# The loads of batch 0 on three queues, token weights held, and a new order of work in a fused attention and wave-MLP kernel

## The chip, the cores and the metric

The kernel runs on one core of a Trainium2 chip. The metric is the device time of one execution in microseconds (us), as a median of several runs. One execution was also taken by the hardware profiler; all views below are of that one. The engines are PE (matrix multiply, with its weight loads as PEld), DVE (elementwise and reductions), ACT (activation functions and copies), POOL (a slower general engine) and SP (which issues transfers). Transfers are moved by 16 DMA engines. SP issues on a queue that the profile calls hardware_dynamic; POOL issues on software_dynamic, and it spends its own time on each issue.

## The reference

Linear attention over 8 batches, 8 heads, 576 positions, 64 values a head, then a norm for each head, then a wave-like MLP over C = 512 channels:

```python
kv  = einsum('bhsd,bhse->bhde', k, v)
out = einsum('bhsd,bhde->bhse', q, kv)
x   = out / sqrt(mean(out*out, -1) + 1e-6) * g_norm      # then (b, s, h*d)
theta = x @ w_theta
y = einsum('ts,bsd->btd', w_tok_r, x*cos(theta)) + einsum('ts,bsd->btd', w_tok_i, x*sin(theta))
u = x + y
result = u + maximum(u @ w_ch, 0)
```

## The kernel before

Each batch has 576 positions, which are cut into four full tiles of 128 rows and one half-size tile (the 64 left-over positions, folded so that 256 columns stand on 128 rows); `j` counts these five. A tile (b, j) goes through these steps, each a small function that issues the instructions of one engine:

- **Attention.** `kv_piece` (L174) multiplies k by v on PE, two heads at a time, four pieces a batch; `kv_out` copies the sum to `kbd` on ACT. `q_turn` (L198) transposes q on PE, `q_out` (L216) copies it to `qT`, `raw` (L222) multiplies `qT` by `kbd`.
- **Norm.** `square` (L243, ACT), `sums` (L249, DVE), `root` (L257, POOL: the lines L260, L264, L266 make `ss`, `rt`, `gr`), `x_make` (L274, DVE: `x = raw * gr`).
- **Phase.** `x_turn` (PE), `x_out` (copy to `xT`), `theta` (PE, with the weights `wth`), `whole_turns` (`pt`), `reduce_arg` and `even_arg` (DVE, L321 and L329), `sine` and `cosine` (ACT), `z_make` (DVE). The half tile's z goes to a buffer `zf` and is moved into place as `zt` by four small transfers on SP (`z_move`, L361).
- **Token and channel mix.** `token_mix` (PE, `y`) sums nine matrix products over all z of the batch; it reads the transposed token weights `wT` (made by `w_turn` and `w_out`) and needs `zt` in its last third. Then `u_make` (DVE), `u_turn`, `u_out`, `channel_mix` (PE, `v`, weights `wch`), `finish` (DVE) and `store` (SP).

The order of the instructions on each engine is fixed before the kernel is built. Every step is a `Task` with an engine, a planned cost, the tasks that it depends on and a key. `in_order` (L35) plays the tasks forward in planned time: of the tasks that can start first on an engine, the one with the smallest key goes next. Keys are counted in tiles: tile (b, j) has `s = 5 b + j`, and its token mix has `s + LAG`. A transfer is a task on its issuing engine plus one on an imagined `wire` that takes `MB` us per megabyte. On the chip each engine runs its list strictly in order and waits for semaphores; a transfer also waits until one of its kind's eight completion semaphores is free, so the ninth transfer on a kind of queue waits for the first to land, and so does everything behind it on its engine.

The transfers at the start, before: SP issues k and v of batch 0 in turn, then `g_norm` (`g8`), then `w_theta` (`wth_s`), then k and v of batch 1. POOL issues q of batch 0, the token weights in six transfers, q of batch 1, `w_ch`, q of batch 2 and 3. `prep_theta` scales `wth_s` into `wth` on ACT. PSUM rings bound how far PE runs ahead: two `raw` tiles, two tiles of transposes, four of the wide sums.

Of the kernel before, what the change touches and what calls it, by code (L numbers as in the profile page):

```python
# [71 lines left out]
def kernel(  # L72
# [78 lines left out]
    IM = S + TL  # L151

    def load_token(w_in, lo, n, at):
        nc.gpsimd.dma_start(
            out=wn[:, :, at:at + n],
            in_=w_in[0:SM, lo:lo + n].rearrange("(p j) s -> p j s", j=NJ),
        )
        nc.gpsimd.dma_start(out=wnt[:, at:at + n], in_=w_in[SM:S, lo:lo + n])
# [279 lines left out]

    def w_turn(n):
        if n < NJ:  # L440
            cols = slice(IM + n, 2 * S, NJ)
        elif n < 2 * NJ:
            cols = slice(n - NJ, SM, NJ)
        else:
            cols = slice(SM, IM)
        t = ps.tile([P, S], FP16, tag="tr", bufs=2, name="wps")
        for jj in range(NJ):
            nc.tensor.transpose(t[:, jj * P:(jj + 1) * P], wn[:, jj, cols], ident[:])
        nc.tensor.transpose(t[:, SM:S], wnt[:, cols], ident[0:TL, 0:TL])
# [35 lines left out]
    for hp in range(NHP):
        hs = slice(2 * hp, 2 * hp + 2)
        a = load("SP", 0.3, lambda hs=hs: load_heads(nc.sync, kt[0], k, 0, hs), key=-49 + hp)
        k_got[0, hp] = load("SP", 0.3, lambda hs=hs: load_heads(nc.sync, vt[0], v, 0, hs),
                            [a.deps[0]], key=-49 + hp + 0.5)
    def load_g():  # L490
        nc.sync.dma_start(out=g8[:], in_=g_norm.unsqueeze(0).broadcast_to((P, D)))
        nc.vector.tensor_scalar(
            out=g8[:], in0=g8[:], scalar1=math.sqrt(D), scalar2=None, op0=ALU.mult
        )

    got["g"] = load("SP", 0.03, load_g, [k_got[0, NHP - 1].deps[0]], key=-41)
    got["wth"] = load(
        "SP", 1.05, lambda: nc.sync.dma_start(
            out=wth_s[:], in_=moe_w_theta.rearrange("(kc p) c -> p kc c", p=P)),
        [got["g"].deps[0]], key=-40)  # L500
    got["tok"] = load("POOL", 2.65, load_tokens, [q_got[0].deps[0]], key=-39)
    sp_prev, pool_prev = got["wth"].deps[0], got["tok"].deps[0]
    w_key = 4.0
# [169 lines left out]
```

## Time and profile before

| | us |
|---|---|
| median of 3 runs (lowest, highest) | 260.32 (260.25, 261.2) |
| profiled execution, its own time | 262.83 |
| profiled execution, span of the trace | 261.0 |
| PE busy in the span | 219.7 |
| POOL, DVE, ACT busy | 135.8, 162.1, 157.0 |

The span runs from the first to the last recorded instruction. The page has the busy time of each engine, the span in 40 slices, the DMA queues, and the chain of work that ended last, followed back from the end to what released each step. The trace also answers for a stretch of time (busy time, granted PE clock, DMA share), for one engine in order of time, and for one tile. A granted clock of 0.50 means that PE ran at half speed; a DMA share over 1 means that more packets were open than there are engines.

### The profile page before, as it was taken

Reading aid. Unit: us, or ns where it says so; the run is one execution under the profiler, and the core shown is the slowest. Engines: PE = TensorE matmul, PEld = TensorE weight load, DVE = VectorE, ACT = ScalarE, POOL = GpSimd, SP = SyncE. Lnnn points to the kernel's source line nnn. Section 1 sums busy time; section 2 is a strip of 40 time slices with the busy share of each in tenths; the row PEclk is TensorE's granted clock in tenths of the full one; section 3 lists DMA queues with packets and bytes.
Section 4 is the critical chain, followed back from the end, with each engine's and each line's share of the span. In section 5 each row is a group of like instructions: output and inputs, shape, how many; then the busy total and the mean of one; then the engine's idle time right before and its main releaser. Section 6 shows DMA issues by size and latency. Waiting matters only on the chain.

```text
span 261.0 us, 5581 instructions
## 1 busy us (share of the span) xinstructions
PE 219.7 (84%) x2221; PEld 126.1 (48%) x2221; DVE 162.1 (62%) x293; ACT 157.0 (60%) x306; POOL 135.8 (52%) x158
## 2 busy tenths in 40 slices
PE   0533055995999989999999999999999999999993
PEld 0433023673644554556555645565556555455551
DVE  3000136626669868976788587958785788964452
ACT  1201529559479857775878587868786877652120
POOL 8442394607975955668466656626571747400000
PEclk9975557589899999999999999999999999999998
DMA  6999999967198399339962596211121112212222
GB/s 110 225 236 261 269 230 239 288 191 216 31 253 209 60 159 316 109 104 113 267 177 102 83 280 201 95 43 40 33 90 43 53 25 87 83 62 86 77 80 100
DMA packets 49449, 37.37 MB, mean 143 GB/s; under 512 B 15504, under 2 KB 44816, under 8 KB 49424
## 3 DMA queue, kind: packets, MB, share of 16 engines
q1 hardware_dynamic: 34400, 30.45, 40.1%
q0 software_dynamic: 15024, 6.57, 20.7%
q8 instruction: 17, 0.28, 0.5%
q14 instruction: 8, 0.07, 0.1%
HBM read 33.10 MB, written 9.44 MB: 163 GB/s over the span
## 4 chain that ended last, share of the span: by engine, by line
PE 66%; DMA 10%; DVE 8%; POOL 8%; ACT 4%; issue 2%; POOLq 0%
PE y L380 22%; DMA qe<-in_q_dram 10%; PE th L297 10%; PE v L297 10%; PE kv L180 6%; PE ups L195 4%; PE y L384 4%; POOL rt L264 3%; PE xps L195 3%; PE qps L203 2%; PE raw L228 2%; DVE x L278 2%; POOL gr L266 2%; PE v L302 2%; DVE arg L321 2%
## 5 line engine op out<-in xcount | busy, mean ns | idle before, releaser
L380 PE MATMUL y<-zm,wT 128*128 128x512 f16 x256 | 69.6, 384 | 0.0
L264 POOL TENSOR_TENSOR rt<-ss,mhalf 128x8 f32<-128x8 f32 (+1 forms) x40 | 62.1, 1554 | 3.3
L260 POOL TENSOR_SCALAR ss<-ss 128x8 f32<-128x8 f32 (+1 forms) x40 | 11.0, 276 | 67.2 <-DVE ss L252 65.9
L266 POOL TENSOR_TENSOR gr<-g,rt 128x512 f32<-128x512 f32 (+1 forms) x40 | 39.6, 991 | 3.1
L278 DVE TENSOR_TENSOR x<-raw,gr 128x512 f16<-128x512 f32 (+1 forms) x40 | 25.3, 632 | 22.6 <-POOL gr L266 22.6
L380 PEld LDWEIGHTS <-wT 128*128 128x128 f16 x288 | 25.1, 99 | 24.6 <-issue 3.6
L297 PE MATMUL th<-wth,xT 128*128 128x512 f16 x128 | 35.6, 406 | 0.8 <-ACT xT L212 0.7
L337 ACT ACTIVATE sc<-arg 128x512 f16<-128x512 f32 (+1 forms) x40 | 23.7, 592 | 16.7 <-DVE arg L321 16.6
L321 DVE SCALAR_TENSOR_TENSOR arg<-pt,th 128x512 f32<-128x512 f32 (+1 forms) x40 | 25.1, 628 | 13.2 <-ACT pt L315 13.1
L212 ACT COPY uT<-ups 128x512 f16<-128x512 f16 (+1 forms) x40 | 21.9, 546 | 19.1 <-PE ups L195 19.0
L180 PE MATMUL kv<-vt,kt 128*64 128x64 f32 x640 | 26.6, 243 | 7.6 <-DMA vt<-in_v_dram 7.6
L297 PE MATMUL v<-wch,uT 128*128 128x512 f16 x128 | 33.0, 380 | 0.0
L315 ACT ACTIVATE pt<-th 128x512 f32<-128x512 f32 (+1 forms) x40 | 22.3, 559 | 14.6 <-PE th L297 14.3
L212 ACT COPY xT<-xps 128x512 f16<-128x512 f16 (+1 forms) x40 | 21.5, 538 | 15.6 <-PE xps L195 15.3
L414 DVE SCALAR_TENSOR_TENSOR ot<-v,u 128x512 f32<-128x512 f32 (+1 forms) x40 | 25.3, 633 | 9.0 <-PE v L297 6.6
L252 DVE TENSOR_REDUCE ss<-sq 128x8 f32<-128x512 f32 (+1 forms) x40 | 24.9, 626 | 8.9 <-ACT sq L246 8.8
L391 DVE TENSOR_TENSOR u<-y,x 128x512 f16<-128x512 f32 (+1 forms) x40 | 25.3, 633 | 7.0 <-PE y L380 5.9
L180 PEld LDWEIGHTS kv<-vt,kt 128*64 128x64 f32 x640 | 23.7, 155 | 11.7 <-issue 10.5
L357 DVE TENSOR_TENSOR zm<-x,sc 128x1024 f16<-128x1024 f16 x32 | 24.3, 758 | 7.1 <-ACT sc L344 7.0
L344 ACT ACTIVATE sc<-arg,quarter 128x512 f16<-128x512 f32 (+1 forms) x40 | 27.1, 676 | 2.5 <-DVE arg L329 2.2
L212 ACT COPY qT<-qps 128x512 f16<-128x512 f16 (+1 forms) x40 | 21.7, 548 | 9.4 <-PE qps L203 9.4
L195 PE MATMUL xps<-ident,x 128*128 128x128 f16 x144 | 15.4, 228 | 10.8 <-DVE x L278 10.7
(53 smaller groups left out, 253.5 us busy)
## 6 DMA issues: line engine op xcount, KB each, us to landing
out_dram<-ot SPq DMA_DIRECT2D x32, 256.0 KB, 2.4
kt<-in_k_dram SPq DMA_DIRECT2D x7, 1024.0 KB, 8.9
vt<-in_v_dram SPq DMA_DIRECT2D x7, 1024.0 KB, 11.7
qh<-in_q_dram POOLq DMA_DIRECT2D x8, 512.0 KB, 7.6
kt<-in_k_dram SPq DMA_DIRECT2D x4, 256.0 KB, 8.1
vt<-in_v_dram SPq DMA_DIRECT2D x4, 256.0 KB, 8.9
wth_s<-in_moe_w_theta_dram SPq DMA_DIRECT2D x1, 1024.0 KB, 12.2
zt<-zf SPq DMA_DIRECT2D x32, 32.0 KB, 1.9
```

What stands on the lines that cost most here:

```text
L180: nc.tensor.matmul(t[i * D:(i + 1) * D, hp, :], kt[b % NKV][:, 2 * hp + i, j, :], vt[b % NKV][:, 2 * hp + i, j, :], start=(j == 0), stop=( ...
L195: nc.tensor.transpose(t[:, i, :], src(i), ident[:])
L212: nc.scalar.copy(out=dst, in_=src)
L264: nc.gpsimd.tensor_tensor(out=rt[:], in0=ss[:], in1=mhalf[:, 0:h], op=ALU.pow)
L266: nc.gpsimd.tensor_tensor(out=gr[:].rearrange("p (h e) -> p h e", h=h), in0=g8[:].unsqueeze(1).broadcast_to((P, h, D)), in1=rt[:].unsqueez ...
L278: nc.vector.tensor_tensor(out=x[:], in0=raw_ps.pop((b, j))[:], in1=gr_sb.pop((b, j))[:], op=ALU.mult)
L297: nc.tensor.matmul(t[:], lhs[:, kc, :], w[:, kc, :], start=first, stop=last)
L321: nc.vector.scalar_tensor_tensor(out=arg[:, 0, :], in0=pt_sb.pop((b, j))[:], scalar=MAGIC, in1=th_ps.pop((b, j))[:], op0=ALU.subtract, op1 ...
L344: nc.scalar.activation(out=sc_sb[b, j][:, 1, :], in_=arg_sb.pop((b, j))[:, 1, :], func=AFT.Sin, bias=quarter[:], scale=-TURN * SHRINK,)
L380: nc.tensor.matmul(t[:], wT[:, w, j * P:(j + 1) * P], r, start=first, stop=last)
L391: nc.vector.tensor_tensor(out=u[:], in0=y_ps.pop((b, j))[:], in1=x_sb.pop((b, j))[:], op=ALU.add)
L414: nc.vector.scalar_tensor_tensor(out=ot[:], in0=v_ps.pop((b, j))[:], scalar=0.0, in1=u_sb.pop((b, j))[:], op0=ALU.max, op1=ALU.add,)
```

## The change

It has these parts. v of batch 0 is issued by ACT, beside k on SP, and `g_norm` goes first on SP. A `Sin` of one column runs on ACT ahead of that. POOL copies one value of v's heads 4 and 5 ahead of the token weights, so that these are issued only when that piece has landed; it scales `g8` there (DVE did), and loads each token matrix in two transfers where there were six in all. q of batch 1 and `w_ch` follow; q of batch 2 and later comes behind the norms of the batch two before it. `prep_theta` moves from ACT to DVE, and `q_out` of batch 0 from ACT to DVE. The last transposes of the token weights (the left-over positions of both matrices) are made in two halves. In the planner, `LAG` falls from 10 to 8, `w_key` rises from 4.0 to 6.3, `square` and `sums` get earlier keys, and transfers get larger planned costs.

```diff
+    warm = const.tile([P, 1], FP32, name="warm")
+    gate = const.tile([1, 1], FP32, name="gate")
...
     def load_tokens():
-        load_token(moe_w_tok_i, 0, SM, IM)
-        load_token(moe_w_tok_i, SM, TL, S)
-        load_token(moe_w_tok_r, 0, S, 0)
+        nc.gpsimd.tensor_copy(out=gate[:], in_=vt[0][0:1, H - 3, 0, 0:1])
+        nc.gpsimd.tensor_scalar(
+            out=g8[:], in0=g8[:], scalar1=math.sqrt(D), scalar2=None, op0=ALU.mult
+        )
+        load_token(moe_w_tok_i, S)
+        load_token(moe_w_tok_r, 0)
...
     def prep_theta(kc):
-        nc.scalar.activation(
-            out=wth[:, kc, :], in_=wth_s[:, kc, :], func=AFT.Copy,
-            scale=UNIT / (2.0 * math.pi),
+        nc.vector.tensor_scalar(
+            out=wth[:, kc, :], in0=wth_s[:, kc, :],
+            scalar1=UNIT / (2.0 * math.pi), scalar2=None, op0=ALU.mult,
         )
...
-    MB = 3.3
+    MB = 3.9
...
+    pool_prev, q_got[0] = load("POOL", 2.3, 1.18, lambda: load_q(0), key=-50)
+    sp_prev, got["g"] = load("SP", 0.5, 0.03, load_g, key=-50)
+    act_prev = None
     for hp in range(NHP):
         hs = slice(2 * hp, 2 * hp + 2)
+        sp_prev, a = load("SP", 1.2, 0.3, lambda hs=hs: load_heads(nc.sync, kt[0], k, 0, hs),
+                          [sp_prev], key=-49 + hp)
+        act_prev, c = load("ACT", 1.2, 0.3, lambda hs=hs: load_heads(nc.scalar, vt[0], v, 0, hs),
+                           [act_prev], key=-49 + hp)
+        k_got[0, hp] = [a, c]
+    sp_prev, got["wth"] = load("SP", 0.5, 1.05, load_wth, [sp_prev], key=-40)
+    pool_prev, got["tok"] = load("POOL", 3.0, 2.65, load_tokens, [pool_prev, *k_got[0, NHP - 2]], key=-39)
+    w_key = 6.3
...
+        add("DVE", 0.5, lambda kc=kc: prep_theta(kc), [got["wth"]], key=1.5)
...
+        pool_prev, q_got[b] = load("POOL", 2.3, 1.18, lambda: load_q(b),
+                                   [last.get(("qt", b - NB, NJ)), last.get(("rt", b - 2, NJ)), pool_prev],
+                                   key=NT * (b - 1) - 6.5)
...
-    LAG = 10.0
+    LAG = 8.0
...
-            t1 = add("ACT", 0.49 * f, lambda b=b, j=j: q_out(b, j, "ACT"),
+            e = "ACT" if b else "DVE"
+            t1 = add(e, 0.49 * f, lambda b=b, j=j, e=e: q_out(b, j, e),
...
             t1 = add("ACT", 0.5 * f, lambda b=b, j=j: square(b, j),
-                     [t, since("ss", b, j, 2)], s + 0.1)
+                     [t, since("ss", b, j, 2)], s - 0.8)
             t2 = add("DVE", 0.6 * f, lambda b=b, j=j: sums(b, j),
-                     [t1, since("rt", b, j, 2)], s + 0.2)
+                     [t1, since("rt", b, j, 2)], s - 0.7)
...
         nc.vector.memset(quarter[:], math.pi / 2)
+        nc.scalar.activation(out=warm[:], in_=quarter[:], func=AFT.Sin)
```

POOL from its first transfer to its first norm, before (`qh`, `qe` are q, `wn`, `wnt` the token weights, `wch` the channel weights; each number behind a name is a buffer):

```order
L141 DMA qh_68<-in_q_dram 128x8x256
L146 DMA qe_71<-in_q_dram 64x4x64 x2
L154 DMA wn<-in_moe_w_tok_i_dram 128x4x512
...
L158 DMA wnt<-in_moe_w_tok_r_dram 64x576
L141 DMA qh_69<-in_q_dram 128x8x256
L146 DMA qe_72<-in_q_dram 64x4x64 x2
L531 DMA wch<-in_moe_w_ch_dram 128x4x512
L141 DMA qh_70<-in_q_dram 128x8x256
L146 DMA qe_73<-in_q_dram 64x4x64 x2
L141 DMA qh_68<-in_q_dram 128x8x256
L146 DMA qe_71<-in_q_dram 64x4x64 x2
L260 TENSOR_SCALAR ss<-ss 128x8
```

The same stretch of POOL in the change:

```order
L143 DMA qh_68<-in_q_dram 128x8x256
L148 DMA qe_71<-in_q_dram 64x4x64 x2
L161 COPY gate<-vt_66 1x1
L162 TENSOR_SCALAR g_90<-g_90 128x64
L154 DMA wn<-in_moe_w_tok_i_dram 128x4x576
L157 DMA wnt<-in_moe_w_tok_i_dram 64x576
L154 DMA wn<-in_moe_w_tok_r_dram 128x4x576
L157 DMA wnt<-in_moe_w_tok_r_dram 64x576
L143 DMA qh_69<-in_q_dram 128x8x256
L148 DMA qe_72<-in_q_dram 64x4x64 x2
L494 DMA wch<-in_moe_w_ch_dram 128x4x512
L263 TENSOR_SCALAR ss<-ss 128x8
```

The copy of `vt` stands ahead of the token weights, and q of batches 2 and 3 (six transfers) no longer stands ahead of the first `ss`.

DVE from its last clearing of a buffer to the second `x` of batch 0, before:

```order
L641 MEMSET kbd_75 128x256
L492 TENSOR_SCALAR g_90<-g_90 128x64
L252 TENSOR_REDUCE ss<-sq 128x8 x2
L278 TENSOR_TENSOR x<-raw,gr 128x512
L252 TENSOR_REDUCE ss<-sq 128x8
L278 TENSOR_TENSOR x<-raw,gr 128x512
```

The same stretch of DVE in the change:

```order
L645 MEMSET kbd_75 128x256
L217 COPY qT<-qps 128x512 x4
L217 COPY qT<-qps 128x256
L255 TENSOR_REDUCE ss<-sq 128x8 x2
L437 TENSOR_SCALAR wth<-wth_s 128x512 x4
L281 TENSOR_TENSOR x<-raw,gr 128x512
L255 TENSOR_REDUCE ss<-sq 128x8
L281 TENSOR_TENSOR x<-raw,gr 128x512
```

The scaling of `wth`, which needs `w_theta` to have landed, now stands ahead of the first `x`, and so do the five copies of q.

ACT from the second transposed `x` (`xT`) to the fourth full tile's `sq`, before:

```order
L315 ACTIVATE pt<-th 128x512
L212 COPY xT<-xps 128x512
L337 ACT_TABLE_LOAD
L337 ACTIVATE sc<-arg 128x512
L344 ACTIVATE sc<-arg,quarter 128x512
L246 ACTIVATE sq<-raw 128x512
L315 ACTIVATE pt<-th 128x512
```

The same stretch of ACT in the change:

```order
L318 ACTIVATE pt<-th 128x512
L215 COPY xT<-xps 128x512
L249 ACTIVATE sq<-raw 128x512
L340 ACTIVATE sc<-arg 128x512
L347 ACTIVATE sc<-arg,quarter 128x512
L318 ACTIVATE pt<-th 128x512
```

`sq` moved ahead of sine and cosine, and the table load stands at the start of the program, ahead of the one-column `Sin`.

More of the change, by code (lines that the diff above doesn't have):

```diff
@@ L433, in prep_theta @@
     def prep_theta(kc):
-        nc.scalar.activation(
-            out=wth[:, kc, :], in_=wth_s[:, kc, :], func=AFT.Copy,
-            scale=UNIT / (2.0 * math.pi),
+        nc.vector.tensor_scalar(
+            out=wth[:, kc, :], in0=wth_s[:, kc, :],
+            scalar1=UNIT / (2.0 * math.pi), scalar2=None, op0=ALU.mult,
         )
     def w_turn(n):
[L440 to L443, printed above, removed]
-        else:
[L445 to L449, printed above, removed]
+        t = ps.tile([P, S], FP16, tag="tr", bufs=2, name="wps")
+        if n < 2 * NJ:
+            at = S if n < NJ else 0
+            parts = [(slice(0, P), slice(at + n % NJ, at + SM, NJ))]
+        else:
+            parts = [(slice(0, TL), slice(SM, S)), (slice(TL, P), slice(S + SM, 2 * S))]
+        for rows, cols in parts:
+            for jj in range(NJ):
+                nc.tensor.transpose(t[rows, jj * P:(jj + 1) * P], wn[:, jj, cols], ident[:])
+            nc.tensor.transpose(t[rows, SM:S], wnt[:, cols], ident[0:TL, 0:TL])
         tr_ps["w", n] = t
@@ L471, in since, with load @@
         return last.get((kind, n // NT, n % NT))
-    MB = 3.3
-    wire = [0.0]
-    def load(queue, mbytes, fn, deps=(), key=0.0):
-        i = add(queue, 0.6, fn, deps, key)
+    MB = 3.9
+    def load(queue, cost, mbytes, fn, deps=(), key=0.0):
+        i = add(queue, cost, fn, deps, key)
         done = add("wire", mbytes * MB, lambda: None, [i], key)
         done.tail = 2.0
-        return done
+        return i, done
     got = {}
-    q_got, k_got, t_got = {}, {}, {}
-    q_got[0] = load("POOL", 1.18, lambda: load_q(0), key=-50)
+    q_got, k_got = {}, {}
@@ L485, with load_g, load_wth, load_wch @@
+    def load_g():
+        nc.sync.dma_start(out=g8[:], in_=g_norm.unsqueeze(0).broadcast_to((P, D)))
+    def load_wth():
+        nc.sync.dma_start(out=wth_s[:], in_=moe_w_theta.rearrange("(kc p) c -> p kc c", p=P))
+    def load_wch():
+        nc.gpsimd.dma_start(out=wch[:], in_=moe_w_ch.rearrange("(kc p) c -> p kc c", p=P))
+    pool_prev, q_got[0] = load("POOL", 2.3, 1.18, lambda: load_q(0), key=-50)
+    sp_prev, got["g"] = load("SP", 0.5, 0.03, load_g, key=-50)
+    act_prev = None
     for hp in range(NHP):
@@ L486 @@
         hs = slice(2 * hp, 2 * hp + 2)
[L487 to L503, printed above, removed]
+        sp_prev, a = load("SP", 1.2, 0.3, lambda hs=hs: load_heads(nc.sync, kt[0], k, 0, hs),
+                          [sp_prev], key=-49 + hp)
@@ L504 @@
+        act_prev, c = load("ACT", 1.2, 0.3, lambda hs=hs: load_heads(nc.scalar, vt[0], v, 0, hs),
[4 more added lines that the diff above has]
+    w_key = 6.3
     theta_ready = [
-        add("ACT", 0.5, lambda kc=kc: prep_theta(kc), [got["wth"]], key=1.5)
+        add("DVE", 0.5, lambda kc=kc: prep_theta(kc), [got["wth"]], key=1.5)
@@ L541 @@
         for hp in range(NHP):
-            t1 = add("PE", 0.62, lambda b=b, hp=hp: kv_piece(b, hp),
-                     [k_got[b, hp], first], NT * b - 2.0 + 0.2 * hp, None if hp else acc_ring)
+            t1 = add("PE", 0.74, lambda b=b, hp=hp: kv_piece(b, hp),
+                     k_got[b, hp] + [first], NT * b - 2.0 + 0.2 * hp, None if hp else acc_ring)
             first = first or t1
```

30 lines of the change are left out of this document (11 added, 19 removed).

## The prediction

> **What bounds the kernel now.** I read the page's 40 slices first, then the busy time by stretches, then each engine in order of time up to the first token mix. In the slices a digit is tenths of 6.5 us; the third row is the clock that PE was granted, the fourth the share of the DMA engines.
>
> ```profile
> PE   0533055995999989999999999999999999999993
> POOL 8442394607975955668466656626571747400000
> PEclk9975557589899999999999999999999999999998
> DMA  6999999967198399339962596211121112212222
> ...
> 0.00:100.00 100.00, 63.42 (x729) 40.48 (x730) 46.63 (x85) 53.98 (x104) 59.59 (x76) 0.81 0.97 202
> 100.00:240.00 140.00, 139.87 (x1382) 77.50 (x1382) 107.43 (x195) 99.69 (x197) 76.19 (x83) 1.00 0.41 109
> ```
>
> The columns of the lower rows are the stretch, its length, busy PE, PEld, DVE, ACT, POOL, granted clock, DMA share and GB/s. From 100 to 240 us PE is busy 139.87 of 140 at full clock, so nothing that this change does to DVE, ACT or POOL there is worth anything unless it makes PE wait. The time to be had lies ahead of 100 us: 36.6 us of idle PE, and more at half clock. The DMA share is at its ceiling until about 50 us, so the start is a question of which bytes come first, and then of who waits for whom:
>
> ```profile
> 17.64 1.50 PE L180 MATMUL kv<-vt,kt 128*64 128x64 f32 x20 [2.99 <-DMA vt<-in_v_dram]
> 23.09 1.34 PE L180 MATMUL kv<-vt,kt 128*64 128x64 f32 x20 [3.95 <-DMA vt<-in_v_dram]
> ...
> 26.51 1.28 DVE L252 TENSOR_REDUCE ss<-sq 128x8 f32<-128x512 f32 x2 [2.30 <-ACT sq L246]
> 34.48 0.69 DVE L278 TENSOR_TENSOR x<-raw,gr 128x512 f16<-128x512 f32 x1 [6.69 <-POOL gr L266]
> ...
> 29.72 0.63 POOL L146 DMA_DIRECT2D qe<-in_q_dram  x1 [5.59 <-DMA qh<-in_q_dram]
> 30.65 0.61 POOL L146 DMA_DIRECT2D qe<-in_q_dram  x1 [0.30 <-DMA qe<-in_q_dram]
> 31.33 0.24 POOL L260 TENSOR_SCALAR ss<-ss 128x8 f32<-128x8 f32 x1
> 34.53 0.24 POOL L260 TENSOR_SCALAR ss<-ss 128x8 f32<-128x8 f32 x1
> 37.77 0.24 POOL L260 TENSOR_SCALAR ss<-ss 128x8 f32<-128x8 f32 x1
> ```
>
> Two things stand one behind the other. The last piece of k and v lands only at 23.09 us. Its first `ss` is ready at 27.15 (26.51 plus half of 1.28), 4.06 us later, but POOL is still issuing q of batches 2 and 3, which waits for earlier transfers to land, and begins the norm at 31.33: 4.2 us lost. The first `x` comes at 34.48.
>
> **The first term: the first x.** What must be moved ahead of it is worked out from the queues:
>
> ```profile
> q1 hardware_dynamic: 34400, 30.45, 40.1%
> q0 software_dynamic: 15024, 6.57, 20.7%
> ...
> 10.00:20.00 10.00, 5.29 (x90) 4.49 (x86) 0.00 (x0) 1.66 (x3) 4.73 (x7) 0.82 1.25 234
> ```
>
> SP's queue took 40.1% of 261 us, 104.7 us, for 30.45 MB: 3.44 us of all engines for a MB. POOL's took 54.0 us for 6.57 MB written, which were 13.1 MB read (it turns f32 into f16): 4.11 us for a MB read. So k or v of a batch (1.18 MB) is 4.06 us, q 4.85, the token weights (2.65 MB) 10.9, `w_theta` 3.6, `w_ch` 4.3; these run down at 1.25 a microsecond. In the change q, k and v of batch 0 go alone, as the token weights wait for heads 4 and 5 of v. That is 12.97 / 1.25 = 10.4 us, and 13 us with the 2.5 us that pass before data flows. The bounds are these 13 us, and 17.64, where the third of four pieces was there before; I take **14 us**, near the lower end, as the wait removes just the 10.9 us that were in between.
>
> From there 4.06 us to the first `ss`: 18.1. POOL's gate opens with the third piece, at about 12; its issues behind it are priced by the same kinds before:
>
> ```profile
> 1.44 1.14 POOL L141 DMA_DIRECT2D qh<-in_q_dram  x1
> 2.58 1.27 POOL L146 DMA_DIRECT2D qe<-in_q_dram  x2
> 3.81 0.75 POOL L154 DMA_DIRECT2D wn<-in_moe_w_tok_i_dram  x1
> 4.55 0.54 POOL L158 DMA_DIRECT2D wnt<-in_moe_w_tok_i_dram  x1
> 16.11 0.75 POOL L531 DMA_DIRECT2D wch<-in_moe_w_ch_dram  x1
> ```
>
> Two token matrices 2.6, q of batch 1 2.4, `w_ch` 0.75, the copy and `g8` some 0.4: POOL is free at about 18.2, just when `ss` is ready, so moving q of batches 2 and 3 behind the norms takes the 4.2 us away whole. The norm takes 3.15 us (31.33 to 34.48), so `gr` is there at 21.3. What is late next is DVE: the four scalings of `wth` now stand ahead of the first `x` and wait for `w_theta`. The change issues that behind the last k piece, at about 11, and 3.6 us of transfer with the token weights beside it puts its landing at 17 to 23; I take 20. DVE's price for such a scaling is not in the trace; the bounds are L329's 0.43 us (quoted below) and ACT's 0.61 for the same work (2.19 for four, one behind the other 0.55); I take 0.43, an operation of one input on DVE. That is 1.7 us, so `x` starts at 22. The q copies on DVE run while it waits for k and v, and cost nothing. **34.48 - 22 = 12.5 us** gained, with ends 9 (17.64 + 4.06 + 3.15 = 24.9, and a little for `wth`) and 13.2.
>
> A rule that speaks against this move stands in the Trainium skill, GPSIMD Engine Reference, Key points: POOL shares its SBUF interfaces with VectorE and contends with DVE instructions that use both ports. The rows show such meetings, each stretching one side:
>
> ```profile
> 39.79 0.43 DVE L329 TENSOR_SCALAR arg<-arg 128x512 int32<-128x512 int32 x1
> 49.68 0.76 DVE L329 TENSOR_SCALAR arg<-arg 128x512 int32<-128x512 int32 x1
> ...
> 33.41 1.04 POOL L266 TENSOR_TENSOR gr<-g,rt 128x512 f32<-128x512 f32 x1
> 39.84 1.28 POOL L266 TENSOR_TENSOR gr<-g,rt 128x512 f32<-128x512 f32 x1
> 49.54 0.61 POOL L266 TENSOR_TENSOR gr<-g,rt 128x256 f32<-128x256 f32 x1
> ```
>
> Once `gr` took 1.28 instead of 1.04, once L329 took 0.76 instead of 0.43. By the rule all four scalings could meet the first norm: 4 x 0.33 + 0.24 = 1.6 us at most, and the first `x` at 23.6; without it, 22. The trace agrees with the rule in these two places; the sum goes without it, and the 1.6 us lie inside the ends above.
>
> **The second term: from the first x to the fifth.** POOL's norms follow each other in 3.2 us (31.33, 34.53, 37.77), then comes this:
>
> ```profile
> 39.67 1.28 ACT L337 ACT_TABLE_LOAD   x1
> 42.12 0.57 ACT L246 ACTIVATE sq<-raw 128x512 f32<-128x512 f32 x1
> ...
> 44.82 0.34 POOL L260 TENSOR_SCALAR ss<-ss 128x8 f32<-128x8 f32 x1 [3.70 <-DVE ss L252]
> 48.11 0.23 POOL L260 TENSOR_SCALAR ss<-ss 128x4 f32<-128x4 f32 x1
> ...
> 50.73 0.41 DVE L278 TENSOR_TENSOR x<-raw,gr 128x256 f16<-128x256 f32 x1
> ```
>
> POOL waited 3.70 us for the fourth `ss`: its `sq` stood on ACT behind the table load, sine and cosine. The change puts `sq` ahead of them and the load at the start, where ACT has nothing else to do than to issue v. If POOL alone sets the pace, four full norms and the half one (48.11 to 50.73 is 2.6) give 4 x 3.2 + 2.6 - 3.15 = 12.3 us from the first `x` to the fifth, against 50.73 - 34.48 = 16.25. I take 12.6: **3.6 us** gained, with ends 0 (the wait comes back elsewhere) and 4.
>
> **The third term: up to the first token mix.**
>
> ```profile
> 50.24 4.17 PE L180 MATMUL kv<-vt,kt 128*64 128x64 f32 x80
> 64.19 1.49 PE L380 MATMUL y<-zm,wT 128*128 128x512 f16 x3
> 69.18 2.55 PE L180 MATMUL kv<-vt,kt 128*64 128x64 f32 x80
> ```
>
> Before, `y` began 13.5 us after the fifth `x`, and k times v of batch 1 was done by then, at half clock. In the change it stands behind the first third of `y`, and the token weights' transposes run between the third and the last theta. The chain that remains (transpose, copy, theta, sine, z, then seven transposes with copies shared by DVE and ACT) I make about 10 us, but 3.4 us of batch 1's PE work (2.55 of it kv at full clock) is left for later. Nothing gained: **0**, ends -3 and 3.
>
> **The rest.** Between 60 and 100 us PE idled 5.0 us (the slices show the dips); the change enters this stretch with less of batch 1 prepared, yet with its q and v long landed. I take 1 us gained, ends -3 and 4. The five more transposes of the token weights cost some 0.3 us. From 100 us on the same work runs on a full PE, 0. Sum: 12.5 + 3.6 + 0 + 1 - 0.3 = 16.8 us. **The span becomes 244.2**; what lies around the span was 262.83 - 261.0 = 1.83, so the profiled execution's own time 246.0. The median of the runs stood 2.51 under it: 243.5, and I say 244.
>
> **The rivals.**
>
> *A wait takes its place: q of batch 1.* It now stands behind 10.9 us of token weights that start at 14. Before, q, token weights and q (20.6 us of transfer) had landed at 29.72, in 27.2 us: 0.76 a microsecond beside SP's queue. At that rate 15.75 us take 20.7 and q lands at 34.7; PE's sixteen transposes of it stand ahead of the fifth `x`'s, which come up at about 36. At half of 1.25 it would land at 39.2, some 4 us late: 248. For it: the margin is one or two microseconds. Against: the rate was read under the same crowding. Chance 0.2.
>
> *More than I count.* PE is granted full clock sooner and batch 1 runs without gaps; the second and third terms at their good ends and 2 us in the rest give 239. Chance 0.12.
>
> *The new order of loads does little.* If the last piece still comes near 19 to 23 us, the 4.2 us of POOL and the second term remain, 7.8 us: 252. The Trainium skill, DMA: Bandwidth & Descriptors, Issuing engines are not separate DMA queues, says that more issuing engines save only the time of issuing; by it v on ACT's queue alone would bring nothing, as here, since the share was at 1.25 already. For the rival speaks only that; against it that the token weights are really held back. Chance 0.07.
>
> *Slower: the moved z comes too late.* With `LAG` 8 a batch's token mix follows its last theta sooner. What that chain takes on the chip:
>
> ```profile
> 157.92 0.63 PE L302 MATMUL th<-wth,xT 128*64 128x256 f16 x8
> 160.85 0.43 DVE L357 TENSOR_TENSOR zf<-x,sc 128x512 f16<-128x512 f16 x1
> 161.30 2.40 SPq L365 DMA_DIRECT2D zt<-zf  x4
> ...
> DMA to landing us min/median/max: 1.7/1.9/6.9
> ```
>
> From the end of theta (158.55) to the landing (163.70 + 1.9) are 7.05 us. In the change's order PE has some 10.5 us of work there (before some 22). With the longest landing, 6.9, the chain is 12.05: 1.5 us of wait in each of seven batches. It decides the sign where a batch waits 16.8 / 7 = 2.4 us, a chain of 12.9; with 3 us it is 21 us of wait, 264. Against it stands the median of 1.9. Chance 0.04.
>
> **How the numbers follow.** Forecast, 240.5 to 247.5: 0.55; q late, 247.5 to 251: 0.2; more, 236 to 240.5: 0.12; little, 251 to 256: 0.07; slower 0.04; what is left, 0.02, near no change. The range is 237.5 to 251, which leaves out some 0.17. Half a per cent is about what a measurement of this kernel can tell from no change; faster by more has 0.95, within it 0.02, slower 0.03.
>
> **What would show it.** The last kv piece of batch 0 at about 14 us and POOL's first norm within half a microsecond of its `ss`; the first `x` at 21 to 24; norms of batch 0 every 3.2 us with no wait of 3 us; the first `y` at 45 to 48; PE full from about 60. Wrong would be: a wait for `wth_s` on DVE beyond 24, q transposes of batch 1 that wait for a transfer, or `y` that waits for `zt` in the steady part.

## The result, and the profile after

The change takes **250.33 us** (median; 249.98 to 250.62), and the kernel before, run beside it, 260.76 (260.25 to 263.58). The ratio is **0.9578, 95% interval 0.9507 to 0.9649**: faster by about 4.2%. The profiled execution of the change took 250.36 us, its span 248.6. From profile to profile the gain is 262.83 - 250.36 = 12.47 us; from median to median 10.4. The profiled execution of the kernel before stood 2.1 us above the median of its runs here, and that of the change at its median, so some 2 us of the 12.4 that are taken apart below may be that one execution's and not the change's.

The slices (now tenths of 6.2 us) and the queues of the changed kernel; a queue's columns are packets, MB, and share of 16 engines:

```profile
PE   0081877999998999999999999999999999999992
...
POOL 5078991019889795863859474748554457700000
PEclk9998597599999999999999999999999999999999
DMA  4999999949159999227941696106530112112223
...
q1 hardware_dynamic: 32736, 29.27, 39.8%
q0 software_dynamic: 14416, 6.57, 20.4%
q10 hardware_dynamic: 1664, 1.18, 1.6%
```

But for single slices, PE is nine tenths busy or more from the eighth slice on (43.5 us), where before it was from the eleventh (65 us). q10 is the new queue, with the 1.18 MB of v of batch 0. To see where the time came from, cut both spans at the same marks of the work: first `x`, fifth `x`, first `y`, then 100 and 240 us. Columns: stretch, length, then busy PE, PEld, DVE, ACT and POOL, granted clock, DMA share, GB/s. The kernel before:

```profile
0.00:34.48 34.48, 8.13 (x122) 7.00 (x122) 4.02 (x11) 7.68 (x14) 17.12 (x29) 0.74 1.14 220
34.48:50.73 16.25, 12.19 (x76) 6.84 (x78) 10.18 (x19) 10.57 (x18) 11.07 (x12) 0.61 1.28 248
50.73:64.19 13.46, 9.87 (x159) 8.00 (x158) 6.88 (x14) 9.27 (x21) 4.18 (x5) 0.88 0.81 234
64.19:100.00 35.81, 33.23 (x381) 18.64 (x379) 25.55 (x44) 26.45 (x53) 27.21 (x31) 0.95 0.72 152
100.00:240.00 140.00, 139.87 (x1382) 77.50 (x1382) 107.43 (x195) 99.69 (x197) 76.19 (x83) 1.00 0.41 109
240.00:261.00 21.00, 16.42 (x118) 8.08 (x112) 8.02 (x14) 3.34 (x7) 0.00 (x0) 0.94 0.25 88
```

The changed kernel:

```profile
0.00:24.06 24.06, 6.40 (x122) 5.71 (x122) 7.06 (x18) 3.30 (x6) 12.27 (x23) 0.98 0.98 237
24.06:36.31 12.25, 8.90 (x57) 4.67 (x58) 9.10 (x16) 8.30 (x16) 11.26 (x13) 0.76 1.25 232
36.31:47.12 10.81, 8.79 (x82) 5.61 (x80) 5.24 (x12) 7.33 (x15) 2.02 (x3) 0.68 1.24 243
47.12:100.00 52.88, 51.09 (x589) 30.51 (x589) 38.13 (x69) 36.67 (x75) 36.53 (x41) 0.97 0.84 208
100.00:240.00 140.00, 138.80 (x1346) 74.60 (x1346) 106.55 (x185) 96.11 (x185) 74.09 (x80) 1.00 0.40 104
240.00:248.60 8.60, 4.04 (x40) 2.12 (x36) 2.85 (x5) 0.96 (x2) 0.00 (x0) 0.98 0.23 76
```

PE is the engine that is busiest, and its idle time and its busy time add up to the span; each stretch gives length minus busy:

| PE idle, us | before | change | gain |
|---|---|---|---|
| to the first `x` | 26.35 | 17.66 | 8.69 |
| to the fifth `x` | 4.06 | 3.35 | 0.71 |
| to the first `y` | 3.59 | 2.02 | 1.57 |
| to 100 us | 2.58 | 1.79 | 0.79 |
| 100 to 240 us | 0.13 | 1.20 | -1.07 |
| rest | 4.58 | 4.56 | 0.02 |
| busy PE, whole span | 219.71 | 218.01 | 1.70 |
| sum | | | 12.4 |

The sum is the 261.0 - 248.6 of the spans. The busy row goes with the clock: the same 122 matmuls ahead of the first `x` took 8.13 us at 0.74 and 6.40 at 0.98, which is 1.73 us. So 10.4 of the 12.4 us lie ahead of the first `x` (8.69 idle and 1.73 busy), and about 1 us was given back in the steady part. The table says where PE lost less time, not which edit did it. From the first to the fifth `x` the span shrank by 4.0 us, but only 0.71 of that is idle time, as PE also had less work there (8.90 us against 12.19).

How the head now runs; these are rows of the changed kernel's engines in order of time (start, duration, engine, line, operation, output from input, count, and in brackets the idle time before and its releaser):

```profile
13.72 0.18 POOL L161 COPY gate<-vt 1x1 f32<-1x1 f32 x1 [9.87 <-DMA vt<-in_v_dram]
14.45 0.83 POOL L154 DMA_DIRECT2D wn<-in_moe_w_tok_i_dram  x1
...
17.91 0.34 PE L183 MATMUL kv<-vt,kt 128*64 128x64 f32 x4 [0.25 <-DMA vt<-in_v_dram]
...
20.92 0.23 POOL L263 TENSOR_SCALAR ss<-ss 128x8 f32<-128x8 f32 x1 [0.87 <-DVE ss L255]
24.11 0.24 POOL L263 TENSOR_SCALAR ss<-ss 128x8 f32<-128x8 f32 x1
...
34.07 0.23 POOL L263 TENSOR_SCALAR ss<-ss 128x4 f32<-128x4 f32 x1
...
21.33 1.42 DVE L437 TENSOR_SCALAR wth<-wth_s 128x512 f16<-128x512 f32 x4
24.06 0.69 DVE L281 TENSOR_TENSOR x<-raw,gr 128x512 f16<-128x512 f32 x1 [1.31 <-POOL gr L269]
36.31 0.41 DVE L281 TENSOR_TENSOR x<-raw,gr 128x256 f16<-128x256 f32 x1
```

POOL is free in time and waits 0.87 us for its first `ss`, where before it came 4.2 us late. The wait of 3.70 us at the fourth norm is gone. DVE's scalings of `wth` end 1.31 us before `gr`, so they cost nothing.

### The profile page after: what moved, and what is told of

It reads as the page before. It is cut to its first block, busy times and chain, and to the rows that moved or that the text cites. A ratio compares the mean times of both kernels' runs of the same rounds, so it can differ in the third digit from the quotient of the medians.

```text
span 248.6 us, 5583 instructions
## 1 busy us (share of the span) xinstructions
PE 218.0 (88%) x2226; PEld 123.2 (50%) x2226; DVE 168.9 (68%) x301; ACT 152.7 (61%) x297; POOL 136.2 (55%) x158
## 3 DMA queue, kind: packets, MB, share of 16 engines
q10 hardware_dynamic: 1664, 1.18, 1.6%
## 4 chain that ended last, share of the span: by engine, by line
PE 72%; POOL 8%; DMA 7%; ACT 6%; DVE 4%; issue 2%; SPq 0%; POOLq 0%
PE y L383 23%; PE v L300 10%; PE th L300 9%; PE kv L183 8%; DMA vt<-in_v_dram 4%; PE y L387 4%; PE ups L198 4%; PE xps L198 4%; POOL rt L267 4%; PE qps L206 3%; POOL gr L269 2%; PE raw L231 2%; DMA kt<-in_k_dram 2%; PE v L305 2%; PE th L305 2%
## 5 line engine op out<-in xcount | busy, mean ns | idle before, releaser
L267 POOL TENSOR_TENSOR rt<-ss,mhalf 128x8 f32<-128x8 f32 (+1 forms) x40 | 63.1, 1577 | 3.3
L263 POOL TENSOR_SCALAR ss<-ss 128x8 f32<-128x8 f32 (+1 forms) x40 | 10.1, 252 | 64.6 <-DVE ss L255 63.7
L269 POOL TENSOR_TENSOR gr<-g,rt 128x512 f32<-128x512 f32 (+1 forms) x40 | 40.4, 1010 | 3.1
L383 PEld LDWEIGHTS <-wT 128*128 128x128 f16 x288 | 24.2, 98 | 23.3 <-issue 3.0
L300 PE MATMUL th<-wth,xT 128*128 128x512 f16 x128 | 34.1, 390 | 1.2 <-ACT xT L215 1.2
L360 DVE TENSOR_TENSOR zm<-x,sc 128x1024 f16<-128x1024 f16 x32 | 25.8, 806 | 3.4 <-ACT sc L347 2.8
L249 ACT ACTIVATE sq<-raw 128x512 f32<-128x512 f32 (+1 forms) x40 | 22.0, 554 | 6.2 <-PE raw L231 6.2
L183 PE MATMUL kv<-vt,kt 128*64 128x64 f32 x640 | 24.4, 234 | 0.2 <-DMA vt<-in_v_dram 0.2
L206 PE MATMUL qps<-ident,qh 128*64 128x128 f16 x256 | 13.7, 238 | 12.3 <-DMA qh<-in_q_dram 12.1
L183 PEld LDWEIGHTS kv<-vt,kt 128*64 128x64 f32 x640 | 21.9, 147 | 4.5 <-issue 3.0
```

What stands on the lines that cost most here:

```text
L183: nc.tensor.matmul(t[i * D:(i + 1) * D, hp, :], kt[b % NKV][:, 2 * hp + i, j, :], vt[b % NKV][:, 2 * hp + i, j, :], start=(j == 0), stop=( ...
L267: nc.gpsimd.tensor_tensor(out=rt[:], in0=ss[:], in1=mhalf[:, 0:h], op=ALU.pow)
L269: nc.gpsimd.tensor_tensor(out=gr[:].rearrange("p (h e) -> p h e", h=h), in0=g8[:].unsqueeze(1).broadcast_to((P, h, D)), in1=rt[:].unsqueez ...
L300: nc.tensor.matmul(t[:], lhs[:, kc, :], w[:, kc, :], start=first, stop=last)
L360: nc.vector.tensor_tensor(out=dst, in0=x[:].unsqueeze(1).broadcast_to((P, 2, w)), in1=sc[:], op=ALU.mult)
L383: nc.tensor.matmul(t[:], wT[:, w, j * P:(j + 1) * P], r, start=first, stop=last)
```

## The experiments

Each of the eleven variants is the changed kernel with the edit shown; the last run, r_after, is the change once more. The medians (us) of e1 to e4, e5 to e8, and e9 to r_after come from three sets of runs on three chips; each ratio is to the kernel before in the same set, whose medians were 262.09, 262.8 and 261.98. Its single runs lie between 259.19 and 264.42, so the ratios tell more than the medians.

| run | median | ratio to before, 95% |
|---|---|---|
| the change | 250.33 | 0.9578 [0.9507, 0.9649] |
| r_after, the change again | 250.88 | 0.9585 [0.9527, 0.9642] |
| e1_not_held | 254.22 | 0.9695 [0.9621, 0.9769] |
| e2_v_on_sp | 252.17 | 0.9647 [0.9599, 0.9694] |
| e3_q_ahead | 260.06 | 0.9938 [0.9892, 0.9983] |
| e4_lag10 | 253.74 | 0.9699 [0.9636, 0.9761] |
| e5_late_sq | 256.62 | 0.9757 [0.9696, 0.9818] |
| e6_wide | 256.86 | 0.9789 [0.9729, 0.9848] |
| e7_kv_early | 252.92 | 0.9606 [0.9558, 0.9654] |
| e8_fill | 249.89 | 0.9498 [0.9454, 0.9543] |
| e9_hold_theta | 257.69 | 0.9852 [0.9788, 0.9917] |
| e10_fill_zt | 257.85 | 0.9853 [0.9796, 0.9911] |
| e11_all | 262.13 | 1.0042 [1.0002, 1.0082] |

### Token weights not held

```diff
     def load_tokens():
-        nc.gpsimd.tensor_copy(out=gate[:], in_=vt[0][0:1, H - 3, 0, 0:1])
```

> The change without the copy of v that holds the token weights, so that POOL issues them as soon as g_norm has landed, at about 5 us. Theory (the hold is what brings k and v of batch 0 early): the last piece of k and v comes at 20 to 23 us in place of 17.9, the first x 2 to 5 us later than 24.06, and the time is 252 to 255. Rival (two hardware queues against POOL's one already protect k and v): last piece within 1 us of 17.9 and the time within 1 us of 250.3.

The token weights are issued from 6.13 us on, and PE waits for the last piece of v; rows of PE and POOL in that run:

```profile
21.71 0.48 PE L182 MATMUL kv<-vt,kt 128*64 128x64 f32 x4 [1.00 <-DMA vt<-in_v_dram]
...
25.07 0.23 POOL L262 TENSOR_SCALAR ss<-ss 128x8 f32<-128x8 f32 x1 [9.70 <-DVE ss L254]
```

The last piece comes 3.8 us later than in the change (21.71 against 17.91), the first `x` at 28.43 instead of 24.06, and the time rises by 3 to 4 us (0.0110 of 262 by the ratio to r_after, 3.9 by the medians). So of the 4.4 us that the hold wins at the first `x`, 3 to 4 stay in the total, and the later last piece says that it works by keeping the token weights away from k and v. In this run `w_theta` landed late too: DVE waited 0.67 us for it, and the longest of the four scalings of `wth`, which ran beside POOL's `gr`, took 1.25 us where the median of the four was 0.43. That is a meeting of POOL and DVE of the kind that the prediction had weighed.

### v of batch 0 on SP's queue

```diff
-        act_prev, c = load("ACT", 1.2, 0.3, lambda hs=hs: load_heads(nc.scalar, vt[0], v, 0, hs),
-                           [act_prev], key=-49 + hp)
+        sp_prev, c = load("SP", 1.2, 0.3, lambda hs=hs: load_heads(nc.sync, vt[0], v, 0, hs),
+                          [sp_prev], key=-49 + hp + 0.5)
```

> The change with v of batch 0 issued by SP again, in turn with k, the token weights still held. Theory (the bytes and the eight semaphores set the landing, not the issuing engine): last piece within 1 us of 17.9, time 249.8 to 251.3. Rival (the second queue is worth something of its own): last piece 2 us or more later and the time 252 or more.

k times v of batch 0 is done at 17.15, a little earlier than in the change (18.25). The first `x` still comes later, at 24.64: the hold opened at 14.66 (13.72 in the change), POOL's issues ran to 20.97, and the first norm began at 21.05, though its `ss` was ready at about 19.7. ACT's queue therefore brings k and v no sooner. The Trainium skill says so (DMA: Bandwidth & Descriptors, Issuing engines are not separate DMA queues): asking from several engines saves only the time of issuing; these landings agree. The time leans the other way: the landing is that of the theory, but 252.17 is the time of the rival, 1.3 us above r_after, and the intervals overlap. The clearest difference that I found on PE is this row:

```profile
54.18 0.38 PE L383 MATMUL y<-zt,wT 128*128 128x512 f16 x1 [1.41 <-DMA zt<-zf]
```

The moved z of batch 0 lands 1.41 us too late here; in the change that wait was 0.0, in r_after 0.41. Whether the second queue is worth anything is not settled.

### q of batch 2 ahead of the norms again

```diff
-                                   [last.get(("qt", b - NB, NJ)), last.get(("rt", b - 2, NJ)), pool_prev],
-                                   key=NT * (b - 1) - 6.5)
+                                   [last.get(("qt", b - NB, NJ)), pool_prev],
+                                   key=NT * (b - 2))
```

> The change with q of batch 2 issued by POOL ahead of the first norm again, as before; its transfers wait for token weights to land, of which the last came at about 30 us. Theory (POOL's order and the early loads are one behind the other, and the early loads are worth nothing without the order): the first norm begins at 30 to 32 us in place of 20.9 and the time is 257 to 261, nearly that of before. Rival (the early loads carry the gain, the order only the 4.2 us that POOL lost before): 253 to 255.

POOL and DVE of that run, in order of time:

```profile
26.26 0.89 POOL L143 DMA_DIRECT2D qh<-in_q_dram  x1 [5.98 <-DMA wn<-in_moe_w_tok_i_dram]
...
30.62 0.62 POOL L148 DMA_DIRECT2D qe<-in_q_dram  x1 [2.83 <-DMA wn<-in_moe_w_tok_r_dram]
31.32 0.23 POOL L263 TENSOR_SCALAR ss<-ss 128x8 f32<-128x8 f32 x1
...
34.46 0.69 DVE L281 TENSOR_TENSOR x<-raw,gr 128x512 f16<-128x512 f32 x1 [11.12 <-POOL gr L269]
```

k and v were in nearly as early as in the change (k times v done at 18.82, there 18.25), yet the first norm stands at 31.32 and the first `x` at 34.46, within 0.02 us of the kernel before (31.33, 34.48). The issue of q waits for the held token weights to land, and the norms wait behind it on POOL. So the hold alone gains nothing at the first `x`: what it wins, POOL loses. The two edits go together. What is left of the gain, 0.6%, is in the stretches behind.

### LAG 10, the lag of before

```diff
-    LAG = 8.0
+    LAG = 10.0
```

> The change with LAG back at 10. Theory (LAG moves work but brings no time, PE being full from 60 us on in either order): 249.3 to 251.3. Rival (the gain, or a loss against the forecast, comes from the closer token mix): 252 or more if it helped, 248.5 or less if it cost.

The head is nearly the same (first `x` 24.62), but from 40 to 50 us PE was granted full clock here, and the first `y` came at 46.07, 1 us sooner than in the change. Stretches of that run, with the columns as above:

```profile
40.00:50.00 10.00, 8.41 (x138) 6.32 (x139) 3.07 (x7) 4.68 (x11) 0.00 (x0) 1.00 1.22 246
...
60.00:70.00 10.00, 7.77 (x132) 5.55 (x131) 7.05 (x13) 7.31 (x15) 7.99 (x10) 1.00 0.01 3
70.00:80.00 10.00, 9.27 (x148) 6.33 (x147) 8.02 (x15) 9.30 (x20) 8.66 (x10) 1.00 1.06 260
80.00:90.00 10.00, 8.95 (x78) 4.67 (x77) 9.17 (x15) 8.28 (x19) 8.02 (x9) 1.00 1.13 271
90.00:100.00 10.00, 7.86 (x68) 4.36 (x67) 8.38 (x16) 7.77 (x16) 8.06 (x10) 0.87 0.95 195
100.00:240.00 140.00, 140.00 (x1349) 76.92 (x1347) 103.85 (x186) 94.16 (x184) 72.08 (x80) 1.00 0.40 106
```

From 60 to 100 us PE idles 6.15 us here and 1.79 in the change; from 100 to 240 it idles 0.00 here and 1.20 there. The difference is 3.2 us in favour of 8, about what the ratios give ((0.9699 - 0.9585) x 261 = 3.0). The intervals just touch, so that there is a gain is likely and not certain. My reading is that, while the pipe fills, a token mix that may go two tiles sooner gives PE work, and that the smaller lag costs a little once it is full.

### Squares and sums with the keys of before, and no Sin ahead

```diff
-                     [t, since("ss", b, j, 2)], s - 0.8)
+                     [t, since("ss", b, j, 2)], s + 0.1)
...
-                     [t1, since("rt", b, j, 2)], s - 0.7)
+                     [t1, since("rt", b, j, 2)], s + 0.2)
...
-        nc.scalar.activation(out=warm[:], in_=quarter[:], func=AFT.Sin)
```

> The change with the keys of square and sums as before and without the one-column sine at the start, so that a table load and a sine and cosine stand ahead of the fourth sq on ACT again. Theory (these carry the second term of the sum): POOL waits 2 to 4 us ahead of the fourth norm, the fifth x comes 2 to 4 us later than 36.3, and the time is 252 to 254. Rival (a later wait hides it, PE being busy with the token weights' transposes at half clock until 47 in any case): the fifth x is later, but the time stays within 1 us of 250.3.

The fourth norm on POOL in that run:

```profile
35.31 0.34 POOL L263 TENSOR_SCALAR ss<-ss 128x8 f32<-128x8 f32 x1 [3.70 <-DVE ss L255]
```

The wait of before is back, to the hundredth, and from first to fifth `x` it takes 16.0 us (24.98 to 40.99). The mechanism of the second term is right; what the keys and the early table load each bring was not taken apart. The time rose by more than that term and beyond the 252 to 254 of the theory (0.0172 of 262 is 4.5 us against r_after). The first `x` was 0.9 us later, k times v of batch 1 ran ahead of the first `y`, for the most part at half clock (4.53 us from 51.03), and PE idled 4.4 us from 70 to 100, against 1.8 in the change; which of these makes up the rest is open.

### k and v of batch 0 in two pieces

```diff
-    for hp in range(NHP):
-        hs = slice(2 * hp, 2 * hp + 2)
+    for hp in range(0, NHP, 2):
+        hs = slice(2 * hp, 2 * hp + 4)
...
-        nc.gpsimd.tensor_copy(out=gate[:], in_=vt[0][0:1, H - 3, 0, 0:1])
+        nc.gpsimd.tensor_copy(out=gate[:], in_=vt[0][0:1, 3, 0, 0:1])
```

> The change with k and v of batch 0 in two pieces of four heads in place of four of two, so that only one of these transfers waits for a semaphore of an earlier one. Theory (in the change a chain of three landings of some 5.5 us each, through reused semaphores, sets the last piece at 17.9 and not the bytes, which would allow 13 to 14): the last piece lands at 13 to 15 us, the first x comes at 21 to 22.5, the time is 247 to 249. Rival (the bytes and latency are the limit): last piece at 17 to 18.5 and 250 to 251.

This was to take out the waits that make the last piece late. The chain of waits of the change shows them (start, duration, what), and its SP queue shows what was issued ahead of that last landing:

```profile
1.18 5.52 DMA kt<-in_k_dram
...
6.72 5.77 DMA vt<-in_v_dram
...
12.51 5.35 DMA vt<-in_v_dram
...
12.62 0.37 SPq L491 DMA_DIRECT2D wth_s<-in_moe_w_theta_dram  x1
```

Each next piece is issued 0.02 us after an earlier transfer has landed, three landings of 5.4 to 5.8 us one behind the other. With two large pieces only the last transfer of v waits in this way (issued at 9.79), and the result is worse: `w_theta` (issued at 6.07), k of batch 1 (8.11) and the token weights (8.87) all run beside q, k and v. The token weights come early because the edit also moved the hold: it waits for the first of two pieces here, where the change waits for the third of four, and opens at 8.15.

```profile
16.85 2.22 PE L206 MATMUL qps<-ident,qh 128*64 128x128 f16 x32 [16.85 <-DMA qh<-in_q_dram]
```

This row of PE is its first: q of batch 0, POOL's first transfer, landed only at 16.85 (12.12 in the change). k times v ended at 23.36, the first `x` came at 29.18. My theory fell: the waits between the pieces also kept the later loads on SP back, and without them, and with the hold open sooner, more bytes shared the engines. How much each of the two lets in was not taken apart.

### Everything later held, with two pieces

```diff
+    def hold():
+        nc.gpsimd.tensor_copy(out=wth_s[0:1, 0, 0:1], in_=vt[0][0:1, H - 3, 0, 0:1])
...
+    pool_prev = add("POOL", 0.6, hold, [pool_prev, got["g"], *k_got[0, NHP - 1]], key=-41)
+    sp_prev, got["wth"] = load("SP", 0.5, 1.05, load_wth, [sp_prev, pool_prev], key=-40)
```

> The change with k and v of batch 0 in two pieces of four heads, g_norm behind them, and POOL's copy of v (of the second piece) written into the buffer of w_theta, so that w_theta and k and v of batch 1 are held too until it is there. In the kernel with wide pieces and the old hold, the hold opened at 8 us and q landed at 16.9. Theory (what delays the last piece in the change is that w_theta, k of batch 1 and the token weights are issued ahead of its landing, so holding all of them leaves the bytes alone): q, k and v landed by 13 to 14.5 us, first x at 21.5 to 23 in place of 24.1, and 0.5 to 2.5 us less than the change. Rival (small loads first, the semaphores' chain, is as good): last piece 16 us or later and no gain.

POOL's copy goes into `wth_s` here, so that `w_theta` and all that SP issues behind it wait for the second v piece too. The hold opened at 13.19. PE then, in order of time:

```profile
14.48 2.22 PE L207 MATMUL qps<-ident,qh 128*64 128x128 f16 x32 [14.48 <-DMA qh<-in_q_dram]
16.45 2.31 PE L184 MATMUL kv<-vt,kt 128*64 128x64 f32 x40
...
18.90 1.39 PE L184 MATMUL kv<-vt,kt 128*64 128x64 f32 x40
```

With no other load on the DMA engines v is in by about 13 and q by 14.5, so the 13 to 14 us of the prediction nearly hold for the bytes. But everything lands at once, PE transposes q and multiplies k by v one behind the other until 20.29, and the first `x` comes at 26.10, 2 us later than in the change, where PE had the pieces from 12 us on. The total rose by far more (7 us by the ratio to r_after); the order of the later work differs and PE idled 2.4 us from 40 to 50 and 3.5 from 70 to 100, of which I did not separate the causes.

### Less planned time for transfers

```diff
-    MB = 3.9
+    MB = 3.3
```

> The change with the planned time of a megabyte back at 3.3, by which k times v of batch 1 is put among the token weights' transposes and its first norms start some 7 us earlier; k and v of batch 1 had landed at 37.5. Theory (the first y comes at the same time but with batch 1 further on): 247 to 249.5. Rival (PE is full from 47 us on and the order of its work there is worth nothing): 249.8 to 251.

k times v of batch 1 moves ahead of the first `y` (44.92, where the change had it at 48.51) and the batch's norms begin at 50.24 instead of 54.95, but the first `y` comes only at 51.57. The time is that of the change within its interval (0.9606 against 0.9578 and 0.9585): the gain of the theory did not come, and a small effect either way is not ruled out.

### Matmuls that nothing reads, to hold the clock

```diff
+    def fill(n):
...
+            nc.tensor.matmul(fill_ps["t"][:], ident[:], wth[:, 0, :], start=True, stop=True)
...
+        if b == 0 and j >= 3:
+            fill(1 if full(j) else 3)
...
+        if n >= 3:
+            fill(1)
```

> The change with some eleven extra 128x512 matmuls, of which nothing is read, ahead of the fourth and fifth theta of batch 0 and behind each later transpose group of the token weights. Theory (PE falls to half clock from 40 to 50.4 us because short waits and transposes alone do not keep it up; matmuls in between do): granted clock near 1.0 in 40 to 50, the first y 2 to 4 us earlier than 47.1, the time 246.5 to 249. Rival (the clock falls all the same): clock 0.5 there, and the extra work makes it 251.5 to 254.

Between 40 and 50 us the change has PE busy at half clock (first fence: its stretch, then PE in order of time); with the extra matmuls, which are ten, it is not (second fence: stretch, PE, and the chain of waits of that run):

```profile
40.00:50.00 10.00, 9.64 (x82) 6.20 (x84) 3.11 (x7) 3.64 (x8) 0.00 (x0) 0.51 1.21 243
...
47.12 1.46 PE L383 MATMUL y<-zm,wT 128*128 128x512 f16 x3
48.51 3.37 PE L183 MATMUL kv<-vt,kt 128*64 128x64 f32 x80
```

```profile
40.00:50.00 10.00, 9.71 (x144) 6.52 (x143) 3.21 (x7) 4.44 (x10) 0.00 (x0) 1.00 1.22 248
...
52.08 0.38 PE L393 MATMUL y<-zt,wT 128*128 128x512 f16 x1 [0.81 <-DMA zt<-zf]
...
45.97 5.98 DMA zt<-zf
```

The clock stays at 1.00, k times v of batch 1 takes 2.55 instead of 3.37, but `y` begins only 0.3 us sooner (46.79), and then PE waits 0.81 us for a moved z whose landing took 5.98. The clock does as the theory said, the first `y` and the time (246.5 to 249) do not. This is the fastest version measured, 249.89 us; by its ratio it leads, but the interval overlaps that of the change, so it is no sure gain.

### The same, with the moved z of batch 0 on ACT's queue

```diff
-                nc.sync.dma_start(
+                (nc.scalar if b == 0 else nc.sync).dma_start(
...
-                t6 = add("SP", 2.4, lambda b=b: z_move(b),
+                t6 = add("SP" if b else "ACT", 2.4, lambda b=b: z_move(b),
```

> The change with the extra matmuls that keep the clock up (as in the run with them) and the moved z of batch 0 issued by ACT in place of SP, where it stood behind v of batch 2. Theory (once PE is at full clock, the first token mix waits for this move, which took 6 us to land behind the loads): it lands in 2 to 3 us, PE waits less than 0.3 us for it, and the time is 1 to 3 us less than the change. Rival (the DMA engines are full, so the queue does not matter): landing 5 us or more, and within 1 us of the run with the extra matmuls alone.

PE still waited 0.62 us for `zt` at 51.55, as the transfers were issued from 43.68 to 46.15 and the last of them took 5.87 us to land, with a DMA share of 1.26 from 40 to 50 us. On SP's queue it had been 5.98, so the queue that asks made no difference there. But the planner then put k and v of a later batch ahead of the moved z of batch 1 on SP; SP's queue and PE in that run:

```profile
80.80 2.68 SPq L137 DMA_DIRECT2D vt<-in_v_dram  x1
83.58 4.25 SPq L378 DMA_DIRECT2D zt<-zf  x4
...
91.23 0.58 PE L393 MATMUL y<-zt,wT 128*128 128x512 f16 x1 [6.05 <-DMA zt<-zf]
```

One late z costs 6.05 us of PE, and from 90 to 100 us the clock is 0.66. It is the wait of the prediction's slower rival, brought about in another way, by transfers that stand ahead of z on SP; in the change no `y` waits for `zt`, and in r_after one does, for 0.41 us.

### Both holds, the fill and the moved z

It is e9_hold_theta and e10_fill_zt together, with no further edit.

> The last two together. Theory (the two shorten one chain one behind the other): the sum of both gains, 2 to 5 us less than the change. Rival (the first norms gain nothing for the first token mix, as the token weights and q of batch 1 then land later): no better than the better of the two.

PE waited 5.68 us for `zt` at 96.28, the first `x` came at 26.29, and the time is within half a per cent of the kernel before. The edits do not add up to a better version.

> The change once more, unaltered, so that the next three kernels stand beside it on one chip. 249.5 to 252.5; its ratio to the kernel before within 0.6% of 0.958.

The change again on the third chip, with no edit: 250.88 us, clock 0.55 from 40 to 50 us, PE idle 1.20 us from 100 to 240. The clock's fall and the small steady loss are there again, and PE waits 0.41 us for a moved z.

## Why the prediction was right, and where its sizes were off

The forecast was 244.0 with a range of 237.5 to 251; 250.33 lies inside, near its upper end, and the sign and both main mechanisms were right: k and v come early, POOL is free for the norms, and the fourth norm no longer waits. The size was not. The time missed the forecast's own band, 240.5 to 247.5 (0.55), and fell into that of the rival in which q of batch 1 is late (247.5 to 251, 0.2), and that wait did not come. So it is the width of the range that holds the result, and it holds it for reasons that the prediction had not named. By its steps:

- **First `x`: right in kind, 2.1 us too early.** Forecast 22 (gain 12.5, ends 9 to 13.2), measured 24.06 (gain 10.4). The step that was mis-sized is "I take 14 us" for the last piece of k and v; it came at 17.91, 3.9 us later and just beyond the upper end that I gave it, 17.64. Two smaller errors took part of that back: from the last piece to the first `ss` it was 2.9 us and not 4.06, mostly because the last wait stood ahead of 4 matmuls (0.34 us) and not of 20 (1.34), and the 0.7 us that I added for `wth` did not come. The bytes would allow 13 to 14.5, as e9 shows, though with all pieces landing together the first `x` came no sooner there. What I left out were the waits between the pieces, three landings of over 5 us in a row: SP and ACT together issued eight transfers by 3.1 us, and the ones behind them waited for earlier ones to land. The DMA share was 0.78 in the first ten microseconds, and `w_theta`, k of batch 1 and the token weights started (12.62, 13.41, 14.45) ahead of the last landing. e6 and e9, with larger pieces, did not gain from fewer waits.
- **POOL in time: right.** I had it free at 18.2 as `ss` came at 18.1; it was free at 20.05, and the norm began at 20.92, when `ss` was there. e3 puts q back ahead of the norms and loses everything at the first `x`. The margin is small: in e2 the hold opened 0.9 us later, and POOL's issues were what the first norm waited for.
- **`wth` on DVE as what is late next: wrong, without effect.** `w_theta` had landed, the four scalings took 1.42 us (I had 1.7), and `gr` was later by 1.31. The meeting of POOL and DVE did not show here; in e1 it did, on one scaling, 0.8 us long.
- **First to fifth `x`: right.** Forecast 12.6, measured 12.25; e5 brings the 3.70 us back.
- **Fifth `x` to first `y`: nearly right.** Forecast 0. It took 2.65 us less, but 3.37 us of k times v of batch 1, partly at half clock, then stood behind the first `y`: -0.7.
- **The rest: wrong in sign.** I had +1 and -0.3. From profile to profile 14.42 us had been gained at the fifth `x` (50.73 - 36.31) and 12.47 in the end: -1.95 for all that came behind, where the forecast has +0.7. Of these 1.07 are the steady part, where I had put 0: DVE's `u` comes late for PE's transposes three times, 1.1 us in all; with `LAG` 10 PE does not wait there (e4, 0.00 idle), but why `u` is late with 8 I did not trace. And the `LAG` edit, which I had priced only through a late z, seems to hold some 3 us of gain, net of that loss (e4); without it the rest would have been about -5.
- **Around the profile: 2.5 us.** I took the median 2.51 us under the profiled execution, as before. The change's profile stood at its median (250.36 and 250.33). One profiled execution of a kernel whose runs scatter from 259.19 to 264.42 is no base for such a correction.

So 250.36 against the forecast's 246.0 for the profiled execution is 2.06 late at the first `x`, 0.35 won on the way to the fifth, 2.65 lost behind it; and the 2.5 of the median stand on top.

Of the rivals, q of batch 1 was in time (PE waits for no transfer of it), the new loads did much, and the late z did not come. "More than I count" asked for full clock sooner and a batch 1 without gaps; the clock fell again from 40 to 50 us, and the steady part had gaps that were not there before.

## What to carry to other kernels

A hold on loads and the order of the engine that issues them are one edit: test the pair, since the held transfers move the wait to whatever stands behind them on the issuing engine. Waits between pieces of a load are not only a loss, as they also keep later loads out of the way; count the bytes that get in when they go. When a load is to land sooner, ask also what the engine behind it does while the pieces arrive: pieces that land together leave it that work for afterwards. When one engine is the bound, cut both spans at the same marks of the work and compare that engine's idle and busy time stretch by stretch: it adds up to the gain, and shows what was given back, though not which edit did it.

## What the runs showed that was not expected

- **Half clock on a busy PE.** From 40 to 50 us PE was busy 9.64 of 10 us at a granted clock of 0.51 (0.55 in r_after), from 41.2 to 47.1 us with transposes alone, and full clock came back about 3.3 us after the wide matmuls of `y` had begun (47.12 to some 50.4). With ten 128x512 matmuls ahead of and among the transposes it stayed at 1.00. But it stayed at 1.00 in the profiled execution of e4 too, which has transposes alone from 41.30 to 46.07 and no such matmuls. So transposes alone do not always bring the clock down, and e8's one trace does not prove that the extra matmuls hold it. The mean clocks of the four runs of each, 0.977 to 0.985 in e8, 0.965 to 0.986 in the change, 0.965 to 0.972 in r_after and 0.954 to 0.980 in e4, speak for some help from them. The Trainium skill (TensorE: Matmul & The Clock Gate, What's actually happening) ties the clock to how busy PE has been, with half clock after an idle window of about 3.4 us. By the profile's busy time there was no such window here: the clock fell at about 40.1 us, when PE had been busy 1.33 of the 3 us from 37 to 40, and stayed low while it was full. The trace fits that rule only if a stretch that is partly busy, or busy with transposes, can count as idle. No run tried either by itself, and it stays open. By the rows of e8 the half clock cost about 1 us, 0.3 ahead of the first `y` and 0.82 in k times v, and the moved z took 0.81 of that back.
- **Small transfers on full engines.** The four small moves of z landed after a median of 1.9 us over the span of before (6.9 at the longest), but the last of batch 0's after 5.98 in e8 with a DMA share of 1.22, and after 5.87 from ACT's queue (e10).
- **A stretched norm.** In the change one `rt` on POOL took 2.33 us (at 74.00) where its like take 1.67, just behind the issue of q. What stretched it is not shown.
